# Sixteen attention pairs beside one plain block of 512 tokens, then two pairs of 448-token blocks with seven products, with weights decoded, split and summed in one tile

## The chip, the cores and the metric

The kernel runs on one core of a Trainium2 chip. The metric is the device time of one execution in microseconds (us). TensorE, VectorE (DVE), ScalarE (ACT), GpSimd (POOL) and the queue of SyncE (SP), which issues every DMA, run side by side and wait for each other by semaphores. Each engine does its instructions in the order in which the program lists them.

## What is computed

Rotary attention over 4 batches, 8 heads, 576 tokens and head size 64, then LayerNorm, an MLP of 512 to 2048 to 512 with ReLU, and a residual:

```python
q_rot, k_rot = rotate(q), rotate(k)
scores = q_rot @ k_rot.T / np.sqrt(64)
attn = np.exp(scores - scores.max(-1)); attn = attn / (attn.sum(-1) + 1e-09)
x = concat_heads(attn @ v)                      # 4 x 576 tokens, 512 wide
xn = (x - mean(x)) / np.sqrt(var(x) + 1e-06) * g_ln
out = x + np.maximum(xn @ w_ch1, 0.0) @ w_ch2   # weights arrive as 64-bit floats
```

## The kernel before

**The order is planned.** The kernel lists its work as tasks (`add`) with the engines that could do each, a duration, what must come first, the ring slots that it takes and gives back, and a priority. `Plan.run` plays the tasks through in time and writes the instructions of each engine in the order that comes out. So a change of priorities, rings or durations moves instructions everywhere.

**Attention** (`attention`) goes through 16 pairs of heads, four to a batch. A pair has nine score units of 128 queries by 576 keys. TensorE makes the scores (L362, L358), DVE their maximum (L388), ACT the exponential (L400). TensorE then transposes the probabilities (L441), with an odd tail of 64 keys transposed apart (L455); ACT or DVE copies them out of PSUM (`copy`, L232). The product with the values is made in two parts (L524, L528), of 256 and of 320 queries, and scaled (L538). The rotation of the next pair's q and k (`prepare`, L330 and L332) is six operations of 128x576 on POOL. The transposes and value products share a ring of two PSUM banks, `t`.

**Weights.** There are 32 units of 512x128 weights. `decode` loads one as 64-bit numbers and makes 32-bit ones: two ACT operations (L679, L682), a shift on DVE (L685), a sum on POOL (L688), a merge of the sign on DVE (L691), and a store to DRAM (`scratch`). Whenever a block needs a unit, `load_w` fetches it into a tile `f` and `split` makes a high and a low half: a cast on ACT (L709) and a difference on POOL or DVE (L713). That is done 32 times for each of three blocks and 24 times for the last two.

**The MLP** works on blocks of tokens. Blocks 0, 1 and 2 (512 tokens) are plain (`mlp_unit`): each unit is 12 matmuls of 512 columns (L820), since the product of split numbers takes three. Blocks 3 and 4 (384 tokens each) are a pair (`pair_stage`): eight stages of seven products instead of eight, each of 12 matmuls of 384 columns (L951), with sums and differences of the operands made on DVE, ACT and POOL (`hidden`, `outputs`, `operand`). The sums of weights for this (`weight_sums`) are made ahead from reloaded quarters, split, and stored in DRAM.

**What sets the order.** The first four pairs run as fast as they can. From the fifth on, a pair's scores are released at a nominal time (`PACE`, `release`), one pair in 9 x 3.4, and plain units, which have the lowest priority, fill TensorE between them. LayerNorm of a block (`layer_norm`) starts when its tokens are through attention. The pair's inputs (`pair_inputs`) are made straight from LayerNorm's tiles in SBUF.

Of the kernel before, what the change touches and what calls it, by code (L numbers as in the profile page):

```python
# [35 lines left out]
BLOCKS = [(0, 512), (512, 512), (1024, 512), (1536, 384), (1920, 384)]  # L36
# [14 lines left out]
PAIRED = [(y, g, i) for y, g in STAGES for i in PRODUCTS]  # L51
FIRST, FAST, PACE = 12.0, 1.4, 3.4
DECODE0, DECODE1 = 70.0, 4.5
RATE = 285.0
EARLY = 30.0
AFTER = 0.0
SLACK = 0.7
WARM = 20
# [113 lines left out]
def rope_attention_then_ln_mlp(  # L172
# [25 lines left out]
    cp, xtp, lnp, hp, wp = pool("const"), pool("xt", RINGS["xt"]), pool("ln"), pool("h", RINGS["h"]), pool("w")  # L198
# [7 lines left out]
    w64p, wsp = passing("w64"), passing("ws", RINGS["ws"])  # L206
# [30 lines left out]
    scratch = {u: dp.tile([P, NC * P], F32, name=f"w{u}") for u in UNITS}  # L237
# [42 lines left out]
    def first_pair():  # L280
        src = qk[0, 0]
        xk = xp.tile([P, 2, S], F32, name="xk")
        xq = xp.tile([P, 2, S], F32, name="xq")
        st["k", 0], st["q", 0] = xk[:, 0], xq[:, 0]
# [22 lines left out]
        ev["qk", 0] = [kk, qq]  # L307
        ev["diag", 0] = [add({"ACT": 0.5}, diagonals(0), [qq, ev["c2"]], nominal(0, 6))]
# [3 lines left out]
    def prepare(i):  # L312
# [856 lines left out]
```

## Time and profile before

| | us |
|---|---|
| three runs, without the profiler | 721.54, 722.12, 726.92 (median 722.12) |
| the profiled execution, device time | 723.35 |
| its span, first to last instruction | 721.6 |
| TensorE busy | 694.2 |
| DVE, ACT, POOL busy | 490.6, 409.0, 416.6 |
| mean granted TensorE clock | 0.988 of full speed |

Busy time is the time in which at least one instruction of the engine was open. For TensorE, whose matmuls overlap, that includes the tail of one that the next does not cover, so a busy TensorE is not one at its peak. A window's row gives busy time and instructions of each engine in that stretch, then the granted clock, the DMA engines' busy share and what they moved.

### The profile page before, as it was taken

The numbers are of one execution on the slowest core, as the hardware profiler recorded it, in microseconds if no ns is written. First come the engines' busy times: TensorE is split into PE (matmuls) and PEld (weight loads), VectorE is DVE, ScalarE is ACT, GpSimd is POOL, SyncE is SP. The second block draws the span as 40 slices with busy tenths as digits, with TensorE's granted clock in tenths as the row PEclk, the third lists the DMA queues.
The fourth block names the chain that finished last, engine by engine and source line by source line (L and its number), as shares of the span: only waits on it lengthen the run. The fifth ranks groups of instructions, "written<-read, shape, count | busy, mean of one in ns | idle before, by whom it ended". The sixth has DMA issues, their size and how long they took to land.

```text
span 721.6 us, 11832 instructions
## 1 busy us (share of the span) xinstructions
PE 694.2 (96%) x4004; PEld 525.6 (73%) x4004; DVE 490.6 (68%) x812; ACT 409.0 (57%) x918; POOL 416.6 (58%) x311
## 2 busy tenths in 40 slices
PE   7999799899999999999999999999999999999998
PEld 5555455677766676887766778877776789899997
DVE  5678767677667966576576856557446475977686
ACT  2676758677678674456566725456545343543430
POOL 4374858376385855456476736665215472764764
PEclk8799999999999999999999999999999999999999
DMA  7284654556766375586667376784311237555564
GB/s 258 74 269 157 221 166 166 169 173 206 241 223 212 102 228 186 178 290 223 193 243 252 124 261 204 251 289 139 111 52 41 71 103 236 173 204 196 174 201 146
DMA packets 73004, 133.57 MB, mean 185 GB/s; under 512 B 11104, under 2 KB 37360, under 8 KB 72944
## 3 DMA queue, kind: packets, MB, share of 16 engines
q1 hardware_dynamic: 72944, 132.82, 54.8%
q8 instruction: 31, 0.51, 0.3%
q14 instruction: 29, 0.24, 0.1%
HBM read 102.83 MB, written 29.96 MB: 184 GB/s over the span
## 4 chain that ended last, share of the span: by engine, by line
PE 85%; DVE 6%; ACT 3%; POOL 2%; issue 2%; DMA 1%; SPq 0%; DVEq 0%; POOLq 0%; ACTq 0%
PE m L820 37%; PE n L951 12%; PE sc L362 10%; PE t L528 9%; PE t L441 8%; PE t L524 2%; PE sc L358 2%; PE t L455 1%; PE t L475 1%; DVE mx L388 1%; POOL o L899 1%; DVE tmp L987 1%; ACT p L400 1%; DMA xk<-in_qk 1%; DMA inv<-sums 1%
## 5 line engine op out<-in xcount | busy, mean ns | idle before, releaser
L713 POOL TENSOR_TENSOR w<-f,w 128x512 fp32r<-128x512 f32 x85 | 113.8, 1341 | 117.3 <-ACT w L709 93.6
L388 DVE TENSOR_REDUCE mx<-sc 128x1 f32<-128x576 f32 x144 | 103.8, 749 | 44.8 <-PE sc L362 32.8
L820 PE MATMUL m<-hh,w 128*128 128x512 f32 x384 | 131.2, 403 | 0.8 <-DVE xt L856 0.8
L820 PE MATMUL m<-xh,w 128*128 128x512 f32 x384 | 130.0, 403 | 0.6 <-ACT bc L232 0.6
L400 ACT ACTIVATE p<-sc,mx 128x576 f32<-128x576 f32 x144 | 106.1, 741 | 37.1 <-DVE mx L388 26.8
L709 ACT CAST w<-f 128x512 fp32r<-128x512 f32 x120 | 73.9, 618 | 76.4 <-PE m L820 68.5
L688 POOL TENSOR_TENSOR d<-d,w 128x512 int32<-128x512 int32 x32 | 42.5, 1332 | 83.8 <-DVE d L685 41.8
L362 PE MATMUL sc<-xk,xq 64*128 64x288 f32 x512 | 86.3, 442 | 2.1 <-DVE xq L293 1.9
L232 ACT COPY pt<-t 128x512 f32<-128x512 f32 (+1 forms) x93 | 51.2, 553 | 63.7 <-PE t L441 59.5
L441 PE MATMUL t<-ident,p 128*128 128x128 f32 x512 | 80.3, 285 | 7.0 <-DVE p L232 1.8
L820 PEld LDWEIGHTS m<-xh,w 128*128 128x128 f32 x384 | 72.9, 190 | 17.8 <-ACT bc L232 1.2
L820 PEld LDWEIGHTS m<-hh,w 128*128 128x128 f32 x384 | 72.3, 188 | 18.3 <-issue 1.9
L441 PEld LDWEIGHTS t<-ident,p 128*128 128x128 f32 x512 | 58.6, 143 | 35.8 <-issue 13.7
L820 PE MATMUL m<-xl,w 128*128 128x512 f32 x192 | 75.5, 393 | 0.0
L820 PE MATMUL m<-hl,w 128*128 128x512 f32 x192 | 75.1, 391 | 0.0
L528 PE MATMUL t<-pt,v 128*64 128x320 f32 (+1 forms) x512 | 69.1, 412 | 0.0
L362 PEld LDWEIGHTS sc<-xk,xq 64*128 64x128 f32 x512 | 48.7, 192 | 20.2 <-issue 8.5
L951 PE MATMUL n<-x,w 128*128 128x384 f32 x336 | 59.6, 335 | 1.8 <-DVE tmp L997 1.2
L951 PEld LDWEIGHTS n<-x,w 128*128 128x128 f32 x336 | 58.3, 188 | 2.9 <-DVE tmp L997 1.5
L856 DVE TENSOR_TENSOR xt<-xt,m 128x512 f32<-128x512 f32 x48 | 32.9, 686 | 40.2 <-PE m L820 40.0
L528 PEld LDWEIGHTS t<-pt,v 128*64 128x64 f32 x512 | 33.9, 136 | 31.3 <-issue 12.3
L232 DVE COPY pt<-t 128x512 f32<-128x512 f32 (+1 forms) x67 | 41.0, 615 | 22.9 <-PE t L441 18.8
(135 smaller groups left out, 1220.1 us busy)
## 6 DMA issues: line engine op xcount, KB each, us to landing
f<-w SPq DMA_DIRECT2D x96, 256.0 KB
s<-ws SPq DMA_DIRECT2D x32, 512.0 KB
w<-s SPq DMA_DIRECT2D x32, 512.0 KB
xk<-in_qk SPq DMA_DIRECT2D x15, 576.0 KB
xq<-in_qk SPq DMA_DIRECT2D x15, 576.0 KB
w<-in_w1p SPq DMA_DIRECT2D x16, 512.0 KB
w<-d SPq DMA_DIRECT2D x32, 256.0 KB
w<-in_w2p SPq DMA_DIRECT2D x16, 512.0 KB
```

The source lines that it names most:

```text
L232: (ACT.copy if plan.engine == "ACT" else DVE.tensor_copy)(o, i)
L362: PE.matmul(ps[:, a, :HS], lhsT=q[r, c * P : (c + 1) * P], rhs=k[r, KEYS[a]], start=True, stop=True)
L388: DVE.tensor_reduce(out=mx, in_=st["ps", i, n][:, :, :HS], axis=AX.XY, op=ALU.max, negate=True)
L400: ACT.activation(out=halves(p), in_=st.pop(("ps", i, n))[:, :, :HS], func=AF.Exp, bias=st.pop(("mx", i, n)), scale=1.0, accum_out=total)
L441: PE.transpose(ps[:, k], p[:, j, j * T + k * P : j * T + (k + 1) * P], ident)
L528: PE.matmul(ps[r], lhsT=v[:, k, r], rhs=pt[:, j, k], start=False, stop=k == 3)
L688: POOL.tensor_tensor(out=z["f"], in0=z["f"], in1=z["c"], op=ALU.add)
L709: ACT.copy(w[:, 0].rearrange("p a n -> p (a n)"), st["f", k].bitcast(F32))
L713: eng().tensor_tensor(out=w[:, 1], in0=st.pop(("f", k)).bitcast(F32), in1=raw(w[:, 0]), op=ALU.subtract)
L820: PE.matmul(ps, lhsT=wt, rhs=x, start=c + m == 0, stop=c + m == NC + 1)
L856: DVE.tensor_tensor(out=o, in0=o, in1=z["ps"][:, :W], op=ALU.add)
L951: PE.matmul(ps, lhsT=wt, rhs=x, start=fresh and kc + z == 0, stop=kc + z == 3, skip_group_check=True)
```

## The change

- **Blocks.** One plain block of 512 tokens and four of 448 in two pairs, (1, 2) and (3, 4). Both pairs come after attention. `PACE` is 2.0 a unit.
- **Weights.** A unit is decoded into one quarter of a tile `fw` that holds four units, split there at once, used by the plain block out of that split tile `w`, and stored split (`split_w`). When four units are there, `weight_sums` makes the sums and differences in place in `fw`, splits them and stores them. The pairs load all weights split: 112 loads of 512 KB, of which 48 are two pieces.
- **LayerNorm of the paired blocks** stores its result to DRAM (`hats`). `pair_inputs` loads it, half the channels at a time, into the one slot of `ln`. The second pair's LayerNorm waits until the first pair's inputs are made, and its inputs use the same tiles as the first pair's, which come free at the sixth of its eight stages.
- **Attention.** The odd tails of two score groups are transposed into one bank and copied in one operation of 256 columns instead of two of 128. The rotated and the swapped half of q and k are tiles of their own.

In the diff a line of "..." marks what is left out.

```diff
-BLOCKS = [(0, 512), (512, 512), (1024, 512), (1536, 384), (1920, 384)]
+BLOCKS = [(0, 512), (512, 448), (960, 448), (1408, 448), (1856, 448)]
...
-RINGS = {"sc": 3, "t": 2, "m": 2, "p": 3, "p9": 1, "pt0": 1, "pt1": 1, "x": 2, "v": 2, "inv": 2, "w64": 2, "f": 3, "d": 2, "w": 6, "h": 4, "xn": 1, "ln": 1, "sq": 2, "xt": 3, "n": 0, "o": 0, "tmp": 0, "ws": 2}
-NPLAIN = 3
-WP = 384
+RINGS = {"sc": 3, "t": 2, "m": 2, "p": 3, "p9": 1, "pt0": 1, "pt1": 1, "x": 2, "xs": 2, "v": 2, "inv": 2, "w64": 2, "fw": 2, "w": 6, "h": 4, "xn": 1, "ln": 1, "sq": 1, "xt": 5, "n": 0, "o": 0, "tmp": 0, "ws": 2}
+NPLAIN = 1
+WP = 448
 LATE = {"n": 6, "o": 13, "tmp": 9}
 BOTH, ROUND = 0.14 + 0.54 * WP / 512, 0.13 + 0.52 * WP / 512
...
-PAIRED = [(y, g, i) for y, g in STAGES for i in PRODUCTS]
-FIRST, FAST, PACE = 12.0, 1.4, 3.4
+PAIRS = [(1, 2), (3, 4)]
+PAIRED = [(y, g, i) for _ in PAIRS for y, g in STAGES for i in PRODUCTS]
+FIRST, FAST, PACE = 12.0, 1.4, 2.0
 DECODE0, DECODE1 = 70.0, 4.5
...
+                x = st["x", i, nm] = [xp.tile([P, S], F32, name=f"x{nm}"), xp.tile([P, S], F32, name="xs", bufs=RINGS["xs"])]
+                st[nm, i] = x[0]
+                for s in range(2):
+                    SP.dma_start(x[s], src[:, 2 * n + s])
...
+            if c % 2 == 0:
+                first_exp = exps[1 + 2 * c]
+                first_trans = trans
+                continue
+
+            def tail(c=c):
+                ps = st["tp", i, c, 2] = tp.tile([P, 512], F32, name="t")
+                for n in range(2):
+                    p = st.pop(("p", i, c - 1 + n))
+                    PE.transpose(ps[:, n * P : (n + 1) * P], p.rearrange("p j s -> p (j s)")[:, S - T : S + T], ident)
+
...
+            dep = trans + first_trans + [exps[2 * c + 1], first_exp]
+            tt = add({"PE": 0.25}, tail, dep, N + 0.3, take=["t"], give=["p", "p"], lag=0.2, name=f"tl{i}.{c}")
+            t2 = add({"ACT": 0.40, "DVE": 0.42}, tail_copy, [tt, parts[a][0]], N + 0.3, give=["t"])
...
-        t1 = add(two, lambda: acc(1), done[0] + done[1], N, take=["ln"], name=f"ln{n}", port=True)
+        t1 = add(two, lambda: acc(1), done[0] + done[1] + ([ev["x made"]] if "x made" in ev else []), N, take=["ln"], name=f"ln{n}", port=True)
...
+                ev["hat", n, c] = add({"SP": 224 / RATE}, lambda c=c: SP.dma_start(hats[n][c], z["xc", c]), [s], N, give=["ln"] if c == NC - 1 else [], name=f"hat{n}.{c}")
...
+            if j == 0:
+                st["fw", k // NC] = fwp.tile([P, NC, NC * P], I32, name="fw")
+            f = z["f"] = st["fw", k // NC][:, j]
...
-        def keep():
-            SP.dma_start(scratch[u], z["f"].bitcast(F32))
...
-        t1 = add({"ACT": 0.67}, a1, [t0], prio, behind=[ev["a1", k - 1]] if k else [], take=["d"])
+        t1 = add({"ACT": 0.67}, a1, [t0], prio, behind=[ev["a1", k - 1]] if k else [], take=["fw"] if j == 0 else [])
...
-        ev["ws", k] = add({"SP": 256 / RATE}, keep, [t5], prio, give=["d"])
-
-    def split(k, there, prio):
...
+        def high():
+            w = st["w", k] = wp.tile([P, 2, NC, P], F32R, name="w")
+            ACT.copy(w[:, 0].rearrange("p a n -> p (a n)"), z["f"].bitcast(F32))
...
+        def low():
             w = st["w", k].rearrange("p h a n -> p h (a n)")
-            eng().tensor_tensor(out=w[:, 1], in0=st.pop(("f", k)).bitcast(F32), in1=raw(w[:, 0]), op=ALU.subtract)
...
+        def keep():
+            r = slice(0 if j < 2 else 2 * P, NC * P)
+            SP.dma_start(split_w[u][:, :, r], raw(st["w", k]).rearrange("p h a n -> p h (a n)")[:, :, r])
+
+        t6 = add({"ACT": 0.62}, high, [t5], prio, take=["w"], behind=[ev["w", k - 1]] if k else [], name=f"w{k}")
+        ev["w", k] = t6
+        ev["wr", k] = [add({"POOL": 1.3, "DVE": 0.68}, low, [t6], prio, port=True)]
+        ev["split", u] = add({"SP": (512 if j < 2 else 256) / RATE}, keep, ev["wr", k], prio)
 
...
+        y, g, i = PAIRED[k - PAIR0]
...
+            w = st["w", k] = wp.tile([P, 2, NC, P], F32R, name="w")
+            w = raw(w).rearrange("p h a n -> p h (a n)")
+            if i not in LEFT:
+                SP.dma_start(w, sums_w[y, g, i])
+                return
+            for h, (u, at) in enumerate(quarter_of(y, g, LEFT[i])):
+                SP.dma_start(w[:, :, 2 * P * h : 2 * P * (h + 1)], split_w[u][:, :, at : at + 2 * P])
...
+        if i in LEFT:
+            there = [ev["split", u] for u, at in quarter_of(y, g, LEFT[i])]
...
+            there = [ev["sums", (y, g)]]
+        ev["w", k] = add({"SP": 512 / RATE}, load, there, prio, behind=[ev["w", k - 1]], take=["w"], name=f"w{k}")
...
+        b = 2 * g + y
+        k0 = NC * b
+        prio = DECODE0 + DECODE1 * (k0 + NC - 1)
...
+        l = [t for k in range(k0, k0 + NC) for t in ev["wr", k]]
...
+        add({"NONE": 0.0}, lambda: None, [t, ev["split", u]], prio, give=["w"])
...
+    def switch1():
+        plain.close()
+        late["x"] = ctx.enter_context(tc.tile_pool(name="late_x", bufs=1, reuse_waits="tile", side="right"))
...
+        prio = XPRIO if q == 0 else XB
...
+            there = [ev["late1"]] if q == 0 else [ev["x made"]]
+            l = []
+            for s, (n, y) in enumerate(((a, c), (a, c + 2), (b, c), (b, c + 2))):
+                def load(s=s, n=n, y=y, z=z):
+                    if s == 0:
+                        z["x"] = lnp.tile([P, NC, BLOCK], F32, name="xc")
+                    SP.dma_start(z["x"][:, s, :WP], hats[n][y])
+
...
+            made.append(add({"NONE": 0.0}, lambda: None, last, prio, give=["ln"]))
+        ev["x made"] = add({"NONE": 0.0}, lambda: None, made, prio)
...
+            if y == 0 and g == 3 and h:
+                give = give + [f"x{c}{i}" for c in range(2)]
...
+    attn = list(plan.tasks)
+    layer_norm(0)
...
+        if k % NC == NC - 1:
+            weight_sums(k // NC % 2, k // (2 * NC))
+    ev["late"] = add({"NONE": 0.0}, switch, attn, 0.0, give=[r for r, n in LATE.items() for _ in range(n)])
...
+    ev["late1"] = add({"NONE": 0.0}, switch1, [t for t in plan.tasks if t not in attn and t is not ev["late"]], 0.0)
+    for q, (a, b) in enumerate(PAIRS):
+        layer_norm(a)
+        layer_norm(b)
+        pair_inputs(q, a, b)
+        for m, (y, e) in enumerate(STAGES):
+            k0 = PAIR0 + (len(STAGES) * q + m) * len(PRODUCTS)
+            for j in range(len(PRODUCTS)):
+                load_w(k0 + j, -2.0)
```

**Where instructions move.** First TensorE at the end of attention, rows before; `n` is a bank of the pair's products, `m` one of a plain unit, `x_0_1` an input of the pair:

```order
L820 MATMUL m<-hl,w 128x512
L820 MATMUL m<-hh,w 128x512 x2
L820 MATMUL m<-hl,w 128x512
L820 MATMUL m<-hh,w 128x512
L951 MATMUL n<-x_0_1_5844,w 128x384 x3
L951 MATMUL n<-x_1_1_5849,w 128x384 x3
L951 MATMUL n<-x_0_1_5844,w 128x384 x3
```

and now; `t` is a bank of attention, `x_4404` and `x_4490` are inputs of the first channels for products 1 and 6, `x_4560` and `x_4582` those of the second:

```order
L504 MATMUL t<-ident,p_4515 128x64 x4
L505 MATMUL t<-ident,p_4515 64x64
L553 MATMUL t<-p_4479,v 128x320
L557 MATMUL t<-pt_4478,v 64x320 x8
L984 MATMUL n<-x_4404,w 128x448 x3
L984 MATMUL n<-x_4560,w 128x448 x3
L984 MATMUL n<-x_4404,w 128x448 x3
L984 MATMUL n<-x_4560,w 128x448 x3
L984 MATMUL n<-x_4490,w 128x448 x3
L984 MATMUL n<-x_4582,w 128x448 x3
L601 MATMUL m<-acc,mean_w 128x448
L602 MATMUL m<-xt_2734,mean_w 128x448
```

The pair followed 168 plain matmuls behind the last attention pair; now it follows attention's last value product directly, with the second pair's LayerNorm (L601, L602) between its products.

Second, POOL in the middle of attention, rows before; `xk` and `xq` are rotations, `d` the decoding sum, `w<-f,w` the split's difference:

```order
L332 TENSOR_TENSOR xk<-xk,rope_sb 128x576 x2
L332 TENSOR_TENSOR xq<-xq,rope_sb 128x576
L713 TENSOR_TENSOR w<-f,w 128x512
L330 TENSOR_TENSOR xk<-xk 128x576
L332 TENSOR_TENSOR xq<-xq,rope_sb 128x576
L713 TENSOR_TENSOR w<-f,w 128x512
L330 TENSOR_TENSOR xq<-xq 128x576
L688 TENSOR_TENSOR d<-d,w_2910 128x512
L688 TENSOR_TENSOR d<-d,w_3020 128x512
L713 TENSOR_TENSOR w<-f,w 128x512
L688 TENSOR_TENSOR d<-d,w_3090 128x512
```

and now; `fw<-fw,w` is the decoding sum, `fw<-fw` a sum of weights, `ws` the split of such a sum, `xc` LayerNorm:

```order
L350 TENSOR_TENSOR xs<-xs,rope_sb 128x576
L782 TENSOR_TENSOR fw<-fw 128x2x256
L348 TENSOR_TENSOR xq<-xq,xs 128x576
L792 TENSOR_TENSOR ws<-fw,ws 128x512
L782 TENSOR_TENSOR fw<-fw 128x2x256 x2
L716 TENSOR_TENSOR fw<-fw,w_2240 128x512
L629 TENSOR_TENSOR xc<-xt_589,bc 128x448 x3
L792 TENSOR_TENSOR ws<-fw,ws 128x512
L716 TENSOR_TENSOR fw<-fw,w_2313 128x512
L736 TENSOR_TENSOR w<-fw,w 128x512
L350 TENSOR_TENSOR xk<-xk,rope_sb 128x576
```

The sums of weights, which stood behind all decoding, now stand between the decoded units.

Third, SP's queue at the end of attention, now; `hat` is a stored LayerNorm result, `sums` and `inv` the sums of a pair's exponentials, `s` a stored sum of weights, `v` a stored split unit:

```order
L535 DMA sums_0_144<-row_4414 4x128
L545 DMA inv<-sums_0_144 64x2x128 x2
L941 DMA xc<-hat_210 128x448 x2
L941 DMA xc<-hat_211 128x448 x2
L535 DMA sums_1_145<-row_4537 5x128
L545 DMA inv<-sums_1_145 64x2x128
L547 DMA inv<-sums_1_145 64x64
L545 DMA inv<-sums_1_145 64x2x128
L547 DMA inv<-sums_1_145 64x64
L754 DMA w<-s_146 128x1024
```

The second half of the first pair's inputs is fetched just ahead of the last pair's sums. Before, no such load existed: the queue held the last reciprocals and then loads of weights.

## Rows read from the trace of the kernel before

**Rows 1.** The page: busy time of each engine, share of the span, instructions

```profile
PE 694.2 (96%) x4004; PEld 525.6 (73%) x4004; DVE 490.6 (68%) x812; ACT 409.0 (57%) x918; POOL 416.6 (58%) x311
```

**Rows 2.** TensorE in order of time: start, duration, line; bracket: idle, releaser

```profile
39.35 0.70 PE L524 MATMUL t<-p,v 128*128 128x320 f32 x2
...
123.92 0.78 PE L524 MATMUL t<-p,v 128*128 128x320 f32 x2
...
131.72 0.33 PE L455 MATMUL t<-ident,p 128*128 128x128 f32 x1 [2.17 <-DVE pt L232]
...
549.97 0.73 PE L524 MATMUL t<-p,v 128*128 128x320 f32 x2
...
714.79 3.29 PE L951 MATMUL n<-o,w 128*128 128x384 f32 x18
```

**Rows 3.** Windows, all engines: stretch, length, PE, PEld, DVE, ACT, POOL, clock, DMA share, GB/s

```profile
39.35:123.92 84.57, 75.17 (x519) 45.35 (x517) 62.95 (x117) 61.64 (x155) 57.19 (x42) 1.00 0.59 198
123.92:274.96 151.04, 147.15 (x892) 101.60 (x891) 110.07 (x190) 107.52 (x244) 94.45 (x66) 0.99 0.58 193
123.92:549.97 426.05, 421.96 (x2413) 305.97 (x2413) 281.17 (x455) 260.59 (x581) 240.62 (x170) 1.00 0.58 194
597.80:721.60 123.80, 118.23 (x673) 116.21 (x671) 91.47 (x152) 48.39 (x96) 72.06 (x59) 1.00 0.56 188
```

**Rows 4.** Windows of the plain matmuls alone (L820)

```profile
123.92:549.97 426.05, 245.49 (x984) 1.00 0.58 194
280.00:320.00 40.00, 38.62 (x169) 1.00 0.65 215
```

**Rows 5.** Window of the pair's matmuls alone (L951)

```profile
640.00:680.00 40.00, 39.65 (x228) 1.00 0.58 197
```

**Rows 6.** Single operations by line: shortest, median, longest ns

```profile
L713 POOL TENSOR_TENSOR w<-f,w x85: 1266/1292/1800, 46.8 to 710.6; 128x512 fp32r<-128x512 f32 x85
L713 DVE TENSOR_TENSOR w<-f,w x35: 646/708/1692, 48.7 to 438.9; 128x512 fp32r<-128x512 f32 x35
L691 DVE SCALAR_TENSOR_TENSOR d<-w,d x32: 670/690/1958, 34.8 to 287.8; 128x512 uint32<-128x512 uint32 x32
L685 DVE TENSOR_SCALAR d<-d x32: 408/418/1203, 29.7 to 285.1; 128x512 uint32<-128x512 uint32 x32
L332 POOL TENSOR_TENSOR xk<-xk,rope_sb x29: 1399/1432/1893, 12.2 to 480.9; 128x576 f32<-128x576 f32 x29
```

**Rows 7.** Window of 123.92 to 274.96: POOL's L332 and L330, DVE's L691, L685

```profile
123.92:274.96 151.04, 31.38 (x20) 0.99 0.58 193
123.92:274.96 151.04, 16.14 (x11) 0.99 0.58 193
123.92:274.96 151.04, 17.04 (x19) 0.99 0.58 193
123.92:274.96 151.04, 10.21 (x20) 0.99 0.58 193
```

**Rows 8.** What TensorE waited for from 40 to 124: us, times, longest

```profile
PE t L441 <- DVE p L232: 1.8, 4, 0.6
PE t L455 <- ACT pt L232: 1.6, 3, 0.7
```

**Rows 9.** Windows, all engines, behind the wait at 131.72, and in the pair's phase

```profile
132.00:134.00 2.00, 2.00 (x7) 1.50 (x6) 2.00 (x5) 1.61 (x4) 1.44 (x2) 0.51 0.00 0
134.00:136.00 2.00, 2.00 (x10) 1.59 (x9) 1.27 (x4) 0.70 (x3) 0.00 (x0) 0.64 0.00 1
...
612.00:627.00 15.00, 13.51 (x77) 12.87 (x76) 13.73 (x19) 8.57 (x18) 12.96 (x11) 1.00 0.55 186
```

**Rows 10.** Difference of an operand, 128x384: shortest, median, longest ns

```profile
L899 DVE TENSOR_TENSOR o<-tmp,o x8: 548/1302/1653, 618.8 to 703.4; 128x384 fp32r<-128x384 f32 x8
L899 POOL TENSOR_TENSOR o<-tmp,o x24: 1010/1160/1341, 614.7 to 704.1; 128x384 fp32r<-128x384 f32 x24
```

**Rows 11.** The window in which DMA moved most, all engines

```profile
440.00:480.00 40.00, 40.00 (x200) 31.96 (x199) 23.54 (x35) 21.42 (x44) 22.83 (x17) 1.00 0.82 276
```

More of the change, by code (lines that the diff above doesn't have):

```diff
@@ L484, in last_copy @@
                 copy(p4[r, 2 * P : 2 * P + T], ps[0:T, 4 * T : 5 * T])
-            tt = add({"PE": 0.42}, last, [exps[8]], N + 0.1 * j, take=["t"], give=["p9"] if j else [], lag=0.2, name=f"tz{i}.{j}")
+            tt = add({"PE": 0.42}, last, [exps[8]], N + 0.1 * j, take=[ring_t(i, j)], give=["p9"] if j else [], lag=0.2, name=f"tz{i}.{j}")
             d = 0.58
-            t2 = add({"ACT": d, "DVE": d + 0.05}, last_copy, [tt, parts[1][0]], N + 0.1 * j, give=["t"])
+            t2 = add({"ACT": d, "DVE": d + 0.05}, last_copy, [tt, parts[1][0]], N + 0.1 * j, give=[ring_t(i, j)])
             parts[1].append(t2)
@@ L729, in load_split @@
-        def load_split():
-            w = st["w", k] = wp.tile([P, 2, NC, P], F32R, name="w", bufs=RINGS["w"])
-            SP.dma_start(raw(w).rearrange("p h a n -> p h (a n)"), sums_w[PAIRED[k - PAIR0]])
-        if k < PAIR0:
-            there = [ev["ws", k % len(UNITS)]]
-        else:
-            there = [ev["sums", PAIRED[k - PAIR0][:2]]]
-            if PAIRED[k - PAIR0][2] not in LEFT:
-                ev["f", k] = ev["w", k] = add({"SP": 512 / RATE}, load_split, there, prio, behind=[ev["f", k - 1], ev["w", k - 1]], take=["w"], name=f"f{k}")
-                ev["wr", k] = [ev["w", k]]
-                return
@@ L741, in load_w @@
-        ev["f", k] = add({"SP": 256 / RATE}, load, there, prio, behind=[ev["f", k - 1]] if k else [], take=["f"], name=f"f{k}")
-        split(k, ev["f", k], prio)
-    def quarters(t, y, g, which):
-        for h in range(2):
-            r, c = divmod(which, 2)
-            if y == 0:
-                u, at = 2 * g + h + 8 * r, 2 * P * c
-            else:
-                u, at = NF + (g // 2 + 2 * c) * NC + h + 2 * r, 2 * P * (g % 2)
-            SP.dma_start(t[:, 2 * P * h : 2 * P * (h + 1)], scratch[u][:, at : at + 2 * P])
@@ L781, in weight_sums @@
-        for n in range(4):
-            l.append(add({"SP": 256 / RATE}, lambda n=n: load(n), [ev["ws", k] for k in range(len(UNITS))], prio, take=["w64"] if n in (0, 2) else [], behind=ev.get("sl", [])))
-            ev["sl"] = l[-1:]
+        l = [t for k in range(k0, k0 + NC) for t in ev["wr", k]]
         s1 = add(how, lambda: tt(3, 2, 3, ALU.add), l, prio, port=True)
@@ L1053, in last @@
                         o = st["xt", n][:, c, :WP]
[L1054 to L1056 removed]
+                        eng().tensor_tensor(out=o, in0=o, in1=st["acc", q, h], op=ALU.add)
+                    ev["xo", n, c] = add({"POOL": 1.3, "DVE": BOTH}, last, [ev["acc", q, h], ev["xo", n, c]], -0.5, port=True)
         elif i == 2:
@@ L1072, in rope_attention_then_ln_mlp @@
     RINGS["xq"] = RINGS["xk"] = RINGS["x"]
+    RINGS.update({f"x{c}{i}": 1 for c in range(2) for i in range(1, 8)})
     c1 = add({"DVE": 0.5}, constants, prio=-100.0)
@@ L1085, in rope_attention_then_ln_mlp @@
     attention_order = []
-    add({"DVE": 0.0}, lambda: None, prio=-95.0, take=["xq", "xk"])
+    add({"DVE": 0.0}, lambda: None, prio=-95.0, take=["xq", "xk", "xs", "xs"])
     add({"SP": 0.1}, lambda: SP.dma_start(g_sb, g), [ev["l_q"]], prio=20.0)
```

249 lines of the change are left out of this document (114 added, 135 removed).

## The prediction

> **What bounds the kernel now.** I read the page's busy times first: TensorE is open 96% of the span, no other engine over 68% [rows 1]. Then TensorE in order of time, to find where pairs end, and windows between those points, which show two regimes. In the first, pairs 2 to 5 of attention run without plain matmuls between them: 84.57 us from the last value product of pair 1 to that of pair 5 (39.35 to 123.92), 21.1 a pair, and TensorE is open only 75.17 of it [rows 2, 3]. In the second, pairs 6 to 16, it is open 421.96 of 426.05 us, since 984 plain matmuls fill it [rows 3, 4]. Behind them come the rest of the plain block and the pair of blocks, 123.80 us with TensorE open 118.23 [rows 3]. So TensorE's work sets the time wherever there is something to fill it with, and the question is what the change does to that work and to the filling.
>
> Then I looked for what the other engines can still take up. The same kind of operation has very different lengths: the split's difference takes 0.65 us at least and 1.69 at most on DVE, 1.27 and 1.80 on POOL; the sign merge on DVE 0.67 and 1.96, a shift 0.41 and 1.20 [rows 6]. The longest is the shortest plus about one operation of the other engine (0.67 + 1.29 = 1.96; 1.27 + 0.53). These are operations that read SBUF tiles on both engines, and they look as if one waited for the other to end. I call the sum of their shortest lengths on both engines the **shared work**. From 123.92 to 274.96 it is: on POOL 66 operations, 31 of them rotations (20 and 11) at 1.43 and 35 at 1.29, together 89.5 us; on DVE 19 at 0.67, 20 at 0.41 and, by the order, 22 others at 0.66, together 35.4 [rows 3, 6, 7]. That is 124.9 of 151.04 us, 83%, the fullest that I found. TensorE was open 97% there.
>
> **The change, part by part.** All sums go against the span of 721.6.
>
> *Matmuls of the MLP.* Where they run closely, 169 plain ones take 38.62 us, 0.2285 each [rows 4], and 228 of the pair's 39.65, 0.1739 each [rows 5]. For 448 columns no row exists; halfway between 512 and 384 columns is 0.2012. Before: 1152 x 0.2285 + 672 x 0.1739 = 380.1. After: 384 x 0.2285 + 1344 x 0.2012 = 358.1. **-22.0**; the bounds of the rate, if all the gain of width were at one end, move it by 1 us.
>
> *Fewer switches.* Between attention's work a plain matmul costs 245.49 / 984 = 0.2495 instead of 0.2285 [rows 4], 0.02 more. 600 of the 984 go, but those are mostly the ones in long runs, which cost little extra, and the 384 that stay are all of the other kind. Between 0 and -12.6: **-4**.
>
> *The end of attention.* By the order the 384 plain matmuls lie between pair 6 and pair 15, with 18 in pair 15 and none in pair 16. A pair with filling costs (426.05 - 984 x 0.2285) / 11 = 18.3 us beside the filling, one without 21.1 [rows 2 to 4]. One and a half pairs lose 2.8 each: **+4** (0 to +6).
>
> *Shared work in attention.* This is the large unknown. Before, the last two blocks' weight sums, and the splits of two more blocks and the pair, ran late, beside long runs of plain matmuls; and `PACE` held pairs 6 to 10 to 30.2 us each (151.04 / 5). Now decoding, splitting and summing all lie inside attention, and POOL's rows show sums between units. By the order, from pair 5's last value product to the last rotation of pair 16 POOL has 62 rotations at 1.43 and 89 others at 1.29, 203.5 us; DVE 22 shifts at 0.41 and 71 others at 0.66, 55.9. Together 259 us. At TensorE's pace this stretch takes 426.05 - 137.1 (600 matmuls) - 4 + 4, less the last pair's 21, = 268. So the shared work would have to run at 97%, where 83% is the fullest seen. At 83% it takes 312 us: +44. At 97% it costs nothing. Which is nearer can't be read from rows; 83% is what was asked for, not a limit seen, because the release of the scores set the pace there and TensorE hardly waited. I take 92% (282 us), **+13**, and keep 0 and +44. DVE alone is no tighter: at the means of the trace, waits included, it has some 250 of 290 us.
>
> *Merged tails.* 64 copies of 128 columns become 32 of 256, and each half of a pair holds the two banks one turn less. In pairs 2 to 5 TensorE waited 1.8 us for tail copies and 1.6 us to start tails [rows 8]; half of that goes, and the rest of the kernel is covered: **-2** (-4 to 0).
>
> *Start of the first pair.* Before, its inputs were ready in SBUF under 168 plain matmuls. Now that cover is gone: SP fetches the second half of the channels only when the first half's last differences are done, during pair 16. Behind that fetch in SP's queue stand the last pair's sums, for which the final scaling on DVE waits, with two differences behind it. Product 1 then needs a rounding and a difference, product 6 three more sums on POOL one after another (1.01 to 1.34 each) and another rounding and difference (0.55 to 1.65 on DVE) [rows 10]. From the fetch that is some 9 to 12 us, of which the last transposes, copies, value product and product 1 cover 8 to 9. And a wait costs twice: behind the 2.17 us wait at 131.72 the granted clock was 0.51 and 0.64 for 4 us [rows 2, 9], 1.7 us of lost work. 0 to +12: **+4**.
>
> *Two pairs instead of one.* Of the pair's 123.80 us, 116.9 are matmuls (672 x 0.1739) and 3.5 the end behind the last one (718.1 to 721.6); 3.4 were lost inside. The second pair repeats that: **+3**. LayerNorm of blocks 3 and 4 and the second inputs now run beside the first pair, whose folds already filled DVE to 13.73 and POOL to 12.96 of 15 us while TensorE fell to 13.51 [rows 9]. 0 to +9: **+3**. The second pair's inputs have two stages (34 us) for two turns of some 12 us, so they should be ready.
>
> *At no cost.* 96 reloads of 256 KB with their casts and differences go; they ran off the path (ACT is idle 42% [rows 1]). The stored LayerNorm results, 16 trips of 224 KB, and the finer loads of q and k hide in SP's queue. The weights of the pairs are 112 x 0.524 = 58.7 MB in 284 us, with the rest 232 GB/s; the trace shows 276 with nothing late [rows 11].
>
> Sum: 721.6 - 22.0 - 4 + 4 + 13 - 2 + 4 + 3 + 3 = 720.6. The profiled execution's device time (723.35) is 1.75 above its span, the median of the three runs (722.12) 1.2 below that, so 0.5 is added: 721. Against the median that is no change: about 1% (7.2 us) is what a measurement of this kernel can tell.
>
> **Rivals.**
> - *All is covered (faster).* Shared work fits at 97%, the pair's inputs come in time, the LayerNorm hides: 721.6 - 26 + 4 - 2 + 3 + 0.5 = 701. For it: TensorE waited only 4 of 426 us in the second regime [rows 3], and attention's pace is now free to be set by whichever engine is last. Against it: 97%.
> - *POOL and DVE bind (slower).* If the shared work stays at 83%, 721 + 31 = 752. It decides from 88% down (294 us, +25: 733). For it: pairs 2 to 5 ran without a pacing release, and still TensorE was open only 89%. The Trainium skill (SBUF — State Buffer, "Who interferes with whom") states the rule for this: DVE with two SBUF inputs and GpSimd exclude each other for a whole instruction. The lengths of rows 6 agree with it. By that rule alone the stretch can't be shorter than the 259 us, which is no loss; its price comes from the waits that two queues in fixed order add.
> - *The weights come too late.* If the pairs' phase got only the 188 GB/s of the old one [rows 3], its 66 MB would take 351 us instead of 284: 788. Nothing in the trace asks for it.
>
> **How the numbers follow.** Forecast (712 to 730) 0.40; all covered (698 to 712) 0.27; POOL and DVE bind (730 to 755) 0.30; late weights 0.03. Predicted 721. The range 702 to 748 leaves a part of the covered case, the upper end of the binding one and the late weights, 0.2 in all. Faster by over 1% is under 714.9: the covered case and a fifth of the forecast, 0.35. Slower is over 729.3: binding, late weights and the forecast's edge, 0.34. The rest, 0.31, is within 1%.
>
> **What would show it.** Matmuls of 448 columns at 0.20 us in the pairs' middle. Pair 5's last value product at about 122, pair 16's near 420 (407 if all is covered, 450 if the shared work binds), and differences on DVE with a mean well above 1 us there. The first of the pairs' matmuls within 3 us of the last value product, then a wait of 2 to 4 us for the inputs of product 6 and a lower granted clock behind it. The rest, from the first pair's start to the end, about 297 us. The forecast is wrong if TensorE waits in pairs 6 to 14 much more or less than 13 us, or if the pairs' phase has waits for DMA.

## The result

| | before | changed |
|---|---|---|
| median without the profiler, 20 runs each | 721.27 us | 713.91 us |
| span of the profiled execution | 721.6 us | 712.2 us |

The ratio is 0.9884, with a 95% interval of 0.9856 to 0.9912: faster by 1.2%, clear of noise, but the interval reaches into the 1% that the prediction counted as no change. The ratio leaves out six of the changed kernel's 20 runs as slow (over 1.5% above its fastest); the medians of all 20 give 0.990. The forecast was 721 us and no change. 714 lies inside its range, but on the faster side, to which it gave 0.35. A second measurement of the same kernel beside the experiments gave 0.986 (0.981 to 0.991).

The page's first line of the changed kernel answers to [rows 1]:

```profile
PE 677.9 (95%) x3908; PEld 515.8 (72%) x3908; DVE 519.2 (73%) x841; ACT 386.9 (54%) x857; POOL 422.3 (59%) x317
```

TensorE in order of time, as in [rows 2] (L553 begins a value product, L984 is the pairs' matmuls), at the last value products of pairs 1, 5, 14 and 16 and at the first matmul of the pairs of blocks:

```profile
37.01 0.81 PE L553 MATMUL t<-p,v 128*128 128x320 f32 x2 [0.24 <-ACT pt L242]
...
119.81 0.78 PE L553 MATMUL t<-p,v 128*128 128x320 f32 x2
...
368.63 0.81 PE L553 MATMUL t<-p,v 128*128 128x320 f32 x2
...
414.78 1.43 PE L553 MATMUL t<-p,v 128*128 128x320 f32 x2 [0.68 <-ACT p L242]
...
420.61 4.06 PE L984 MATMUL n<-x,w 128*128 128x448 f32 x18
```

The windows between these points (columns as in [rows 3]):

```profile
0.00:37.01 37.01, 27.54 (x167) 19.43 (x167) 25.26 (x50) 18.92 (x46) 16.75 (x18) 0.91 0.56 190
37.01:119.81 82.80, 73.92 (x513) 45.02 (x513) 62.94 (x110) 61.26 (x152) 62.41 (x45) 1.00 0.59 190
119.81:368.63 248.82, 245.49 (x1539) 169.17 (x1539) 193.84 (x313) 177.05 (x405) 184.57 (x132) 0.99 0.60 210
368.63:414.78 46.15, 39.02 (x244) 23.98 (x243) 28.03 (x47) 28.66 (x73) 20.09 (x16) 0.96 0.55 180
414.78:712.20 297.42, 291.93 (x1450) 258.21 (x1450) 209.11 (x323) 101.00 (x184) 138.43 (x109) 0.99 0.67 214
```

The kernel before, cut at the same pairs: windows of pairs 6 to 14 and of pairs 15 and 16:

```profile
123.92:493.59 369.67, 365.78 (x2057) 265.26 (x2057) 254.30 (x408) 229.30 (x506) 224.00 (x158) 1.00 0.62 209
493.59:549.97 56.38, 56.18 (x358) 40.70 (x357) 26.87 (x47) 31.29 (x77) 16.62 (x13) 1.00 0.29 95
```

And the changed kernel's matmuls alone, plain (L831) in pairs 6 to 14, then the pairs' (L984) in their middle:

```profile
119.81:368.63 248.82, 99.29 (x366) 0.99 0.60 210
...
640.00:680.00 40.00, 40.00 (x196) 1.00 0.66 211
```

From these rows the 9.4 us between the two spans can be laid out by the prediction's own terms. A plain matmul counts 0.2285, one of 384 columns 0.1739, one of 448 columns 40.00 / 196 = 0.2041. Before, pairs 6 to 14 hold 876 plain matmuls and pairs 15 and 16 hold 108; after, 366 and 18. LayerNorm's matmuls are shown apart because they moved: before, 9.8 us of them lie in pairs 6 to 14, 4.0 in pairs 15 and 16, 4.1 behind; after, 10.3, 0 and 9.0.

| term | forecast | measured | from |
|---|---|---|---|
| pair 1 | 0 | -2.3 | 39.35 to 37.01 |
| pairs 2 to 5 (merged tails) | -2 | -1.8 | 84.57 to 82.80 |
| matmuls of the MLP | -22 | -18.0 | 380.1 to 87.7 + 274.3 |
| pairs 6 to 14 beside plain matmuls: switches -4, shared work +13 | +9 | -4.8 | 369.67 - 200.2 - 9.8 to 248.82 - 83.6 - 10.3 |
| pairs 15 and 16 (end of attention) | +4 | +14.3 | 56.38 - 24.7 - 4.0 to 46.15 - 4.1 |
| from there to the end, beside the MLP (start, second pair, LayerNorm) | +10 | +1.8 | 171.63 - 155.3 - 4.1 to 297.42 - 274.3 - 9.0 |
| LayerNorm's matmuls | in the above | +1.4 | 17.9 to 19.3 |

Three terms were far off: +9 that was -4.8, +4 that was +14.3 and +10 that was +1.8. The first two nearly cancel, which is luck.

### The profile page after: what moved, and what is told of

The parts are those of the page before. It is cut to its first block, busy times and chain, and to the rows that moved or that the text cites. A ratio compares the mean times of both kernels' runs of the same rounds, so it can differ in the third digit from the quotient of the medians.

```text
span 712.2 us, 11490 instructions
## 1 busy us (share of the span) xinstructions
PE 677.9 (95%) x3908; PEld 515.8 (72%) x3908; DVE 519.2 (73%) x841; ACT 386.9 (54%) x857; POOL 422.3 (59%) x317
## 4 chain that ended last, share of the span: by engine, by line
PE 85%; DVE 5%; ACT 4%; DMA 3%; SPq 1%; issue 1%; POOL 0%; DVEq 0%; ACTq 0%
PE n L984 38%; PE m L831 11%; PE sc L380 10%; PE t L557 8%; PE t L465 7%; PE t L553 2%; PE sc L376 2%; DMA xs<-in_qk 1%; ACT pt L242 1%; DVE mx L412 1%; PE t L485 1%; ACT p L424 1%; PE t L504 1%; DMA inv<-sums 1%; DVE fw L719 1%
## 5 line engine op out<-in xcount | busy, mean ns | idle before, releaser
L984 PE MATMUL n<-x,w 128*128 128x448 f32 x672 | 142.7, 369 | 1.3 <-POOL x L918 0.7
L984 PEld LDWEIGHTS n<-x,w 128*128 128x128 f32 x672 | 125.2, 188 | 16.0 <-issue 3.1
L984 PE MATMUL n<-o,w 128*128 128x448 f32 x576 | 120.0, 368 | 0.0
L984 PEld LDWEIGHTS n<-o,w 128*128 128x128 f32 x576 | 108.1, 188 | 10.6
L911 ACT ACTIVATE o<-tmp 128x448 fp32r<-128x448 f32 x96 | 54.6, 578 | 99.3 <-PE n L984 42.6
L918 POOL TENSOR_TENSOR o<-tmp,o 128x448 fp32r<-128x448 f32 x58 | 74.7, 1315 | 31.1 <-ACT o L911 31.1
L716 POOL TENSOR_TENSOR fw<-fw,w 128x512 int32<-128x512 int32 x32 | 43.0, 1349 | 59.0 <-ACT w L710 32.0
L1056 DVE TENSOR_TENSOR xt<-xt,n 128x448 f32<-128x448 f32 x80 | 48.6, 616 | 21.4 <-PE n L984 21.0
L831 PE MATMUL m<-xh,w 128*128 128x512 f32 x128 | 48.2, 418 | 0.0
L831 PE MATMUL m<-hh,w 128*128 128x512 f32 x128 | 47.1, 414 | 0.0
L350 POOL TENSOR_TENSOR xs<-xs,rope_sb 128x576 f32<-128x576 f32 x29 | 46.4, 1600 | 0.2 <-DMA xs<-in_qk 0.2
```

The costliest lines, as they stand in the source:

```text
L350: eng().tensor_tensor(out=x[step], in0=x[step], in1=rope_sb[:, step], op=ALU.mult)
L831: PE.matmul(ps, lhsT=wt, rhs=x, start=c + m == 0, stop=c + m == NC + 1)
L911: ACT.activation(out=o[0], in_=x(), func=AF.Relu if relu else AF.Copy)
L918: eng().tensor_tensor(out=lo, in0=x(), in1=raw(hi), op=ALU.subtract)
L984: PE.matmul(ps, lhsT=wt, rhs=x, start=fresh and kc + z == 0, stop=kc + z == 3, skip_group_check=True)
L1056: DVE.tensor_tensor(out=o, in0=o, in1=ps(which, h), op=ALU.add)
```

## The experiments

Ratios are against the kernel before; the changed kernel's 0.9884 is the mark to compare with.

**Control.** The changed kernel, unaltered.

> The changed kernel once more, unaltered, as the control for the kernels beside it, since the first four pairs of the last runs differed by up to 7 us between kernels that are the same up to pair 15 (the granted clock rose from 0.50 at 18 us in one and at 28 in another). 0.984 to 0.992 of the time of before; if the clock of the first 30 us is chance, pair 1 ends somewhere between 35 and 44 us here too.

Measured: 0.986 (0.981 to 0.991), span 709.3. Pair 1 ended at 36.5 us. Pairs 2 to 5 took 82.82 us, pairs 6 to 14 248.02, pairs 15 and 16 44.77, the rest 297.18. So a stretch repeats to about 1 us, except where the clock dips (pair 15 here without its dip: 1.4 less). Over all profiles of kernels with the changed first pair, pair 1 ended between 35 and 44 us; the -2.3 us of pair 1 lie within that and prove nothing.

**Less shared work.**

```diff
-eng().tensor_tensor(out=view(o), in0=view(a), in1=view(b), op=op)
+eng().tensor_tensor(out=view(o)[:, :, :16], in0=view(a)[:, :, :16], in1=view(b)[:, :, :16], op=op)
```

> The changed kernel with the four additions and subtractions of each block's weight sums done on 16 of each 128 columns only (the rest of the sums is left out; every instruction stays in its place). That takes some 35 us of the 247 us of POOL's and DVE's shared work between pair 5 and the last rotation of pair 16, so 81% of the stretch instead of 95%. By the prediction's term (13 us lost at a full stretch, nothing at 83%) -10 to -13; if all of it is covered, as the waits of pairs 7 to 14 say (1.2 us), 0 to -2.

Measured: 0.992 (0.988 to 0.995), no gain. The window of pairs 6 to 14 in this kernel:

```profile
118.85:365.49 246.64, 243.73 (x1539) 168.45 (x1539) 183.06 (x313) 176.77 (x405) 162.99 (x132) 1.00 0.61 212
```

The kernel leaves out most of the sums' work: at the shortest lengths of these operations in the trace some 24 us less (the 35 that were expected were too many), and with less waiting for each other POOL is busy 21.6 us less and DVE 10.8. These nine pairs are shorter by 2.2 us than in the changed kernel, by 1.4 than in the control. So the sums cost 1 to 2 us at most where they stand.

**More shared work**, by the differences of the sums' splits written twice, and by all differences written twice:

```diff
+            for _ in range(2):
                 eng().tensor_tensor(out=part(n, 1), in0=view(n), in1=raw(part(n, 0)), op=ALU.subtract)
```

> The changed kernel with the difference of every sum's split written twice, in the same order: 14 more operations of 1.28 us on POOL and 12 of 0.68 on DVE in the same stretch, 26 us, so 273 us of shared work in 261. With both differences doubled (53 us more) the time grew by some 40. If the cost starts where the stretch is full, here 12 to 16; if it is proportional, 20; if it starts well above 100%, 0 to 5.

> The changed kernel with every split's difference (of decoded weights and of sums) written twice, in the same order on every engine. That adds 29 operations of 1.28 us on POOL and 23 of 0.68 on DVE between pair 5 and pair 16's last rotation, 53 us on top of some 247 in a stretch of 261. If the two engines exclude each other in these operations, the stretch must grow to at least 300: +39 or more (+65 at the 92% of the prediction). If they don't, POOL alone has 242 us in 261, and the time grows by 0 to 5.

Measured: 1.020 (1.016 to 1.025) and 1.050 (1.046 to 1.054), so 3.2 and 6.1% more than the changed kernel, 23 and 44 us. The windows of pairs 6 to 14 and of pairs 15 and 16, first with the sums' differences doubled:

```profile
124.55:389.81 265.26, 251.92 (x1538) 170.16 (x1538) 213.43 (x323) 177.58 (x405) 209.07 (x146) 0.98 0.58 197
389.81:440.58 50.77, 41.64 (x243) 25.64 (x243) 32.80 (x51) 28.44 (x73) 20.42 (x16) 0.90 0.51 166
```

then with all doubled:

```profile
133.56:410.18 276.62, 252.69 (x1538) 169.64 (x1538) 230.25 (x334) 177.44 (x406) 229.63 (x160) 0.99 0.54 189
410.18:462.46 52.28, 43.64 (x243) 26.53 (x242) 32.56 (x51) 28.62 (x73) 22.00 (x17) 0.87 0.49 160
```

TensorE's work is the same in all of them, 366 plain matmuls among it. Counted in each trace from pair 5's last value product to the end of the last rotation (operations that start in it), at the lengths of the prediction (1.43, 1.29, 0.41 and 0.66 us). The last column is the share of the stretch in which at least one of these operations was open on either engine, as recorded:

| kernel | rotations and others on POOL | shifts and others on DVE | shared work | stretch | share | open |
|---|---|---|---|---|---|---|
| changed | 56, 83 | 22, 70 | 242.4 us | 261.3 us | 93% | 86% |
| sums' differences twice | 56, 97 | 22, 82 | 268.4 us | 278.0 us | 97% | 89% |
| all differences twice | 56, 112 | 22, 93 | 295.0 us | 291.1 us | 101% | 93% |

The 26 us of the first step lengthen the stretch by 16.8, the 53 of both by 29.8; more is lost in pairs 2 to 5 (5.9 and 6.8), where some of the doubled work lies too and the clock dipped (0.94 and 0.97), and in pairs 15 and 16 (4.6 and 6.1). So the engines do take turns. That is all but free at 93%, and of what comes on top two thirds of the first step and half of the second show up in the stretch. The bound of "at least 300" was not reached: the share goes to 101%, at least in part because the recorded lengths of neighbours on one engine overlap by 0.03 to 0.08 us (as in the rows at the end), and by the last column neither engine had such an operation open in 7% of the fullest stretch. The edge lies somewhere between the changed kernel's 93% and 97%; no run places it closer.

**Filling later.** Plain unit k is held until score group 25 + 49k/31, or 25 + 51k/31, so that the filling reaches further towards the end:

```diff
-ahead = [ev["m", k - 1]] if k else []
+ahead = ([ev["m", k - 1]] if k else []) + [attention_order[25 + k * 49 // 31]]
```

> The changed kernel with plain unit k held back until score group 25 + 49k/31 has started (a floor only): 30 plain matmuls instead of 18 lie in pair 15, fewer in pairs 9 to 13, where TensorE waits for nothing. If the 7 us of waits in pairs 15 and 16 and the lowered clock behind them come from the lack of filling, -1 to -3 (pair 15's 3.4 us of waits go first); if they are latencies that filling doesn't hide, 0.

> The same with 51k/31: 36 plain matmuls in pair 15 and 12 in pair 16, the last ones some 13 us later. The waits of pairs 15 and 16 (7.1 us) and the clock behind them (2 to 5 us) should go, but the first pair's inputs can only be loaded when the last plain product is done (396 us in the changed kernel, 24 us ahead of their first use). If attention's last pair was the cover that they need, a wait of 5 to 10 us appears ahead of the first products, and the sum is 0 to +4; if they had time to spare, -5 to -8.

Measured: 0.999 (0.996 to 1.003) and 1.010 (1.006 to 1.014), both slower than the changed kernel. Pairs 15 and 16 beside plain matmuls did get shorter, 37.6 (44.50 - 30 x 0.2285) and 37.3 (48.22 - 48 x 0.2285) instead of 42.0. But see TensorE at the start of the first pair, 30 matmuls in pair 15:

```profile
426.53 1.50 PE L984 MATMUL n<-x,w 128*128 128x448 f32 x6
431.50 6.79 PE L984 MATMUL n<-x,w 128*128 128x448 f32 x24 [3.47 <-DVE xt L567]
```

and 36 in pair 15, 12 in pair 16:

```profile
422.38 0.88 PE L984 MATMUL n<-x,w 128*128 128x448 f32 x3
428.65 4.42 PE L984 MATMUL n<-x,w 128*128 128x448 f32 x12 [5.40 <-ACT x L911]
435.01 0.47 PE L984 MATMUL n<-x,w 128*128 128x448 f32 x1 [1.94 <-ACT x L911]
```

In the second, what is missing are the inputs of the pair, as the first case of its expectation has it, though that case put the sum at 0 to +4 and the span was 15.8 us longer; in the first, TensorE waits for the late final scaling on DVE (L567), which by the program hands back a bank. From the last value product to the end the two took 301.8 and 310.4 us instead of 297.4. Pairs 6 to 14, thinner in filling now, lost too: TensorE waits 7.5 and 10.9 us there (3.3 in the changed kernel). In the second kernel pairs 1 to 5 took what they take in the changed one, so the loss is the edit's; of the 11.5 us that the first one's span is longer, 7.4 lie in pairs 1 to 5, whose code is the same and where the clock was lower. The empty end of attention is the cover under which the first pair's inputs are made.

**The clock at the end of attention.** Two small matmuls that feed nothing stand ahead of each group of transposes and value product there:

```diff
+ps = bank()
+for k in range(2):
+    PE.matmul(ps[:, k * P : (k + 1) * P], lhsT=ident, rhs=ident, start=True, stop=True)
```

> The changed kernel with two 128-column matmuls into a spare bank, read by nobody, ahead of each group of transposes and each value product in the second half of pair 15 and in pair 16 (some 19 places, 0.16 us each matmul, 6 us in all, mostly inside the 7.1 us of waits). If the granted clock fell there because TensorE waited, it stays near 1.00 between 388 and 424 (it was 0.50 to 0.80 in five stretches of 4 us) and 5 us come back, less 1 to 2 us of matmuls that fit in no wait: -3 to -4, 708 to 709. If the clock has another cause, it stays low and the time grows by 0 to 2.

Measured: 0.998 (0.995 to 1.002), slower than the changed kernel. In the changed kernel the granted clock (the third last column) around the last value product, windows of 4 us, TensorE alone:

```profile
412.00:416.00 4.00, 2.44 (x13) 0.76 0.71 205
416.00:420.00 4.00, 4.00 (x17) 0.50 0.16 52
420.00:424.00 4.00, 4.00 (x20) 0.89 0.08 20
```

and with the extra matmuls, where the last value product starts at 424.46:

```profile
420.00:424.00 4.00, 3.81 (x36) 1.00 0.35 110
424.00:428.00 4.00, 3.96 (x24) 1.00 0.40 122
428.00:432.00 4.00, 2.42 (x12) 1.00 0.28 85
432.00:436.00 4.00, 2.67 (x8) 0.85 0.22 87
436.00:440.00 4.00, 4.00 (x14) 0.72 0.00 0
```

The clock stayed up while TensorE had something to do and fell about 10 us later, behind two waits for DVE (1.6 and 1.3 us). Pairs 15 and 16 took 48.19 us instead of 46.15: the matmuls cost more than the clock gave back. These 2 us and 0.8 behind them are the edit's; the rest of the loss lies in pairs 1 to 5, whose code is the same, and stays unexplained beyond the chance of the clock there.

**The blocks of before in the changed kernel.**

```diff
-BLOCKS = [(0, 512), (512, 448), (960, 448), (1408, 448), (1856, 448)]
+BLOCKS = [(0, 512), (512, 512), (1024, 512), (1536, 384), (1920, 384)]
-PAIRS = [(1, 2), (3, 4)]
+PAIRS = [(3, 4)]
+SP.dma_start(raw(w).rearrange("p h a n -> p h (a n)"), split_w[u])   # plain blocks 1, 2
```

> The blocks of before (three plain ones of 512, one pair of 384) with the changed attention, decoding, split store, sums and merged tails; plain blocks 1 and 2 load their split weights, 512 KB a unit, instead of splitting again. If each term stands as the two traces give it: 1152 x 0.2285 + 672 x 0.1739 = 380.1 of matmuls instead of 362.0 (+18), but pairs 15 and 16 are filled (7 us of waits and 5 us of lowered clock go, -12) and no second pair starts (-3 to -7): about 711 of span, as fast as the changed kernel. Rival: the matmuls of the two pairs are what made the change faster; then the time is that of before or more, 720 to 730.

Measured: 1.044 (1.039 to 1.048), far from the 711 us expected. TensorE behind the plain block:

```profile
604.35 0.39 PE L841 MATMUL m<-hh,w 128*128 128x512 f32 x1
612.03 1.60 PE L994 MATMUL n<-x,w 128*128 128x384 f32 x3 [7.30 <-ACT x L921]
621.83 3.99 PE L994 MATMUL n<-x,w 128*128 128x384 f32 x12 [8.19 <-ACT x L921]
627.50 0.44 PE L994 MATMUL n<-x,w 128*128 128x384 f32 x1 [1.68 <-ACT x L921]
```

17.2 us of waits for the inputs, and a granted clock of 0.67 (604 to 616) and 0.61 (616 to 632). In this kernel the inputs can only be made behind the last plain product, and nothing covers them. The run therefore doesn't compare the blocks, but it prices the cover; what the blocks are worth stays a sum of rows (the -18.0 above), not a run. It also shows attention with the new weights and filling to its end: 323.42 us with 534 plain matmuls, 201.4 beside them; before, 426.05 - 984 x 0.2285 = 201.2. Its last two pairs:

```profile
384.13:443.67 59.54, 59.54 (x351) 43.04 (x350) 24.86 (x47) 26.71 (x64) 4.04 (x3) 1.00 0.39 130
```

126 plain matmuls, so 30.8 beside them, where the changed kernel has 42.0: no wait at all, and a clock of 1.00.

**Tails.** Undone in the changed kernel; put alone into the kernel before; and copied in two pieces in the changed kernel's order.

```diff
-dep = trans + first_trans + [exps[2 * c + 1], first_exp]
+dep = trans + [exps[2 * c + 1]]
```

> The changed kernel with each score group's tail transposed and copied by itself again (64 copies of 128 columns). By the prediction's term +2; pairs 1 to 5 were 4.1 us shorter after the change, and if all of that is the tails, +4: 714 to 716 of span. If the tails are nothing, pairs 2 to 5 stay at 82.8 us and pair 1 at 37.0. The planner also ends the filling one pair earlier here (none in pair 15), which may add 2 to 5 in pairs 14 and 15; the first five pairs are the clean measure.

> The kernel before with the merged tails alone. By the prediction's term -2 and by the tails_undone run (17 us slower than the changed kernel) -10 to -15. If -10 or more comes out, the merged tails alone make the kernel faster and the two pairs of blocks with the new handling of the weights bring nothing; if 0 to -4, the tails matter only where attention runs without filling, and the 17 us were the planner's other order.

> The changed kernel with each merged tail copied by two copies of 128 columns, in the same order and still from one bank: 32 more copies, some 5 us more on ACT or DVE in all (a copy of 128 columns takes 0.26, one of 256 0.40). By the term for the tails about half of its 2 us, in pairs 2 to 5; if copies were what made the tails_undone run 17 us slower, +5 or more.

Measured: 1.013 (1.009 to 1.017), 1.005 (1.002 to 1.009) and 0.990 (0.987 to 0.994). Undoing costs 18 us, but the merge alone brings the kernel before nothing, and the copies are not it. In the first, pairs 2 to 5 carry it:

```profile
41.73:135.70 93.97, 82.18 (x533) 49.45 (x533) 71.54 (x124) 70.10 (x174) 66.85 (x46) 0.96 0.54 180
```

11.2 of the 18.3 us by which the span is longer: 2.9 more of waits and 8.3 more of open time, with the clock at 0.96 and the last step of block 0's LayerNorm here instead of in pair 6. Another 4.7 lie in pair 1, where the clock dipped. The edit changes the order that the planner finds in all of attention, and no run separates that from the tails. What the merge is worth by itself stays open, between nothing (the kernel before with it) and 18 us.

**The first 30 us.** Thirty instead of twenty of the matmuls that run ahead of the first scores.

> The changed kernel with 30 instead of 20 of the matmuls that TensorE runs ahead of its first scores (they feed nothing), everything else in the same order. In eight profiles of kernels with the same first pair these ended 2.2 to 3.8 us before the first scores, the granted clock was 0.50 from about 12 us on and rose again between 18 and 30 us, and pair 1 ended between 35.9 and 44.0 us; that is most of what two runs of one kernel differ by. If the clock falls because of that first wait, it now stays high and pair 1 ends near 35 in every run: -3 to -5, 708 to 710, with less spread. If the 1.7 us wait behind the first scores is enough, nothing changes; the extra 3 us of matmuls then cost 0 to 1.

Measured: 0.985 (0.980 to 0.989), the fastest of all kernels here, but not told apart from the changed one. The granted clock in the changed kernel

```profile
12.00:16.00 4.00, 2.30 (x10) 0.50 0.93 344
16.00:20.00 4.00, 3.59 (x15) 0.74 0.37 143
```

and with the longer lead

```profile
12.00:16.00 4.00, 2.29 (x18) 1.00 0.96 366
16.00:20.00 4.00, 2.86 (x16) 1.00 0.22 85
...
92.00:96.00 4.00, 3.23 (x16) 0.53 0.12 36
```

The early dip is gone and pair 1 ends at 34.35 us, the earliest seen. Another dip came at 92 us, which the changed kernel's two profiles don't have, and pairs 2 to 5 took 85.37 instead of 82.80.

## Why the prediction came out as it did

**The span came out 8.4 us below the sum** (712.2 instead of 720.6). The time lies in the range, though the terms that made it do not stand as forecast.

*Shared work, +13.* This was the step that failed, and by the prediction's own sign: TensorE was to wait about 13 us in pairs 6 to 14, and it waits 3.3, against 3.9 before. The exclusion was right: doubling the work shows it, and its price. Two things were wrong. The need was too high, 259 us instead of 242: the trace has 56 rotations and 83 others on POOL behind pair 5's end, not 62 and 89, because some lay ahead of it. With 242 us even the forecast's 92% would have asked for 263.5 us, where the stretch took 261.3. And "I take 92%" was no limit either: it would have given the two kernels with doubled work 292 and 321 us, and they took 278 and 291. The prediction said itself that 83% was what was asked for and not a limit, and still placed its loss between it and the need. The waits of the changed kernel in pairs 6 to 14 are mostly

```profile
PE t L553 <- DVE p L242: 2.1, 2, 1.8
PE m L651 <- DVE hl L858: 0.5, 1, 0.5
```

(us, times, longest), none for a rotation or for weights. TensorE set the pace to the end, so queues that wait for each other only used up their slack. The rival with +31 is refuted, and with it the point where it decides, 88%. The sign of differences on DVE "well above 1 us" came out at the edge: 23 of them, 1.01 on average.

*Fewer switches, -4.* The size fits, since with the shared work at nothing the -4.8 of pairs 6 to 14 are all that is left for this term. That the switches made it isn't shown. Pairs 6 to 14 of three_plain, then of the kernel before with merged tails:

```profile
120.25:384.13 263.88, 256.67 (x1580) 177.46 (x1581) 202.61 (x319) 187.28 (x425) 197.76 (x139) 0.99 0.64 225
```

```profile
121.66:485.52 363.86, 360.74 (x2037) 263.84 (x2036) 251.03 (x388) 226.58 (x497) 211.87 (x152) 0.99 0.64 214
```

The second has 864 plain matmuls, almost as many as before, and only 155.7 us beside them and LayerNorm (10.8), close to the changed kernel's 154.9. The first has 408, almost as few as the changed kernel, and 159.8 (LayerNorm 10.9), as many as before (159.7), though 3.9 of that are waits that the changed kernel doesn't have. So the number of plain matmuls does not decide it alone, and where the 4.8 us come from stays open.

*End of attention, +4.* Mis-sized: +14.3, and mostly on the side of the kernel before. The forecast took 18.3 us for each of the two pairs when filled, the mean of eleven, and 2.8 more for one and a half of them: 40.6 in all. They took 42.0, so the cost of a pair without filling was about right. But before, the last two pairs took 27.7, or 31.7 with LayerNorm, and not 36.6; and these 4.0 us of LayerNorm moved behind attention. In three_plain, too, the last filled pairs are cheap (30.8 for both). What makes the empty pairs dear is in part what the forecast had seen in pairs 2 to 5, waits: 7.1 us, mostly for copies out of PSUM and for the scaling that frees a bank,

```profile
PE t L465 <- DVE xt L567: 1.7, 2, 1.0
PE t L465 <- DVE pt L242: 0.9, 1, 0.9
PE sc L376 <- ACT p L424: 0.8, 1, 0.8
PE t L504 <- DVE pt L242: 0.8, 1, 0.8
```

and the clock drops to 0.50 (1.2 GHz) behind them, at 390 and at 414 us, which the forecast had counted only for the pair's start.

*Start of the first pair, second pair, LayerNorm, +10.* Too dear: +1.8. The first product follows the last value product without a wait (420.61; 5.8 us behind the start of that product, not 3, since it ran at the clock of 0.50), and products 1 and 6 meet none: the second half of the inputs came in time. The 3 us that the clock cost in 414.78 to 430 (mean 0.80) are the end of attention's doing. The second pair's start shows no wait over 0.75 us. The later filling shows why the prediction's worry was right in kind: with 51k/31 the inputs are fetched 14 to 16 us later, and the products wait 7.3 us.

*Matmuls, -22.* -18.0: 448 columns cost 0.2041, not the 0.2012 halfway between 384 and 512. The changed kernel at 384 columns (three_plain) gives 39.66 / 229 = 0.1732, so it is the width and not the surroundings. The bound of 1 us was too narrow: with the cost per column of either end it is 2 us, and the measured rate lies outside that, too.

*Tails, -2.* -1.8 in pairs 2 to 5, but whether the tails did it is not shown: in the kernel before with the merge alone these pairs took 85.4 us, not less than 84.6 (its clock there was 0.98).

From the first pair's start on about 297 us were foretold; from 420.61 it took 291.6, the matmuls 4 longer than foretold, the rest 9 shorter. (The 297.4 of the window begin at the last value product; that the figures are alike means nothing.) Pair 16's end was forecast near 420, or 407 if all is covered; it was 414.8, all covered and the end of attention dearer.

## What to carry to other kernels

A share of an exclusive resource that a trace shows is what was asked of it, not a limit. While another engine sets the pace, price the resource by what is left of the stretch: here nothing up to 93%, then half to two thirds of what is added. Find the edge by doing work twice that can be done twice without harm, in an unchanged order, and count the need between the same two points in every engine's trace. Work that is no longer filled costs its waits and the slower clock behind them; compare it with the very pieces that it replaces, not with a mean over all filled ones. But before filling it, see what it covers. Two terms of a sum that are each 10 us off can give the right answer, so check the terms, not only the total.

## What the runs showed of the hardware

**The exclusion holds for one-input operations too, and not for those that read PSUM.** DVE in the changed kernel, then POOL at the same time:

```profile
258.60 0.67 DVE L858 SCALAR_TENSOR_TENSOR hl<-m,hh 128x512 fp32r<-128x512 f32 x1
259.20 1.12 DVE L713 TENSOR_SCALAR fw<-fw 128x512 uint32<-128x512 uint32 x1
260.24 1.90 DVE L719 SCALAR_TENSOR_TENSOR fw<-w,fw 128x512 uint32<-128x512 uint32 x1
```

```profile
258.72 1.31 POOL L716 TENSOR_TENSOR fw<-fw,w 128x512 int32<-128x512 int32 x1
260.00 1.59 POOL L350 TENSOR_TENSOR xk<-xk,rope_sb 128x576 f32<-128x576 f32 x1
261.55 1.85 POOL L350 TENSOR_TENSOR xs<-xs,rope_sb 128x576 f32<-128x576 f32 x1
```

L858 reads a PSUM bank and one SBUF tile and takes its usual 0.67 beside L716 (0.67 to 0.69 in all 16 of the stretch above). The shift L713 (0.41 alone) ends 0.29 us behind the end of L716, L719 (0.67 alone) 0.55 behind the end of the first L350, and the second L350 (1.40 alone) is held up by 0.45 until L719 ends. The Trainium skill (SBUF — State Buffer, "Who interferes with whom") says so of both, and counts the shift's kind (`tensor_scalar`) among the operations that can enter a faster mode which takes the shared pair; the trace agrees.

**The clock's dips decide what one run shows.** In the profiles the granted clock fell to 0.50 behind waits of TensorE, single ones (2.2 us at 132 in the kernel before, 7.3 in three_plain) or several short ones (0.6, 0.8, 0.4 and 0.7 us around the drop at 414), at the start and mostly where attention isn't filled, and a dip lasted 3 to 20 us, at about half the speed (the second part of the last value product took 4.54 us instead of 2.38); the same code at the same place had one in some runs and not in others. Pair 1 alone varied by 9 us. For a change of 1% a stretch must be compared with a stretch of the same clock, and a single span proves little.
